# Opening of a windowed-attention and two-layer kernel reordered: sums apart from products, first-layer tiles by pair, scores further ahead, keys loaded first

## The chip, the cores and the metric

One core of one Trainium2 chip. The time is the device time of one execution in microseconds (us), the median of several. `PE` is TensorE, `PEld` its weight loads, `DVE` VectorE, `ACT` ScalarE, `POOL` GpSimd, `SP` the engine that issues most transfers. In the prediction, SWDGE means the transfers that GpSimd issues (here the weights) and HWDGE those that SP issues (here the inputs). PSUM is the memory that TensorE writes its results to (`s`, `x`, `mm`, `ps` and `tp` below are tiles of it).

A line of a timeline gives start and duration in us, engine, line of the kernel, operation, tile written <- tiles read, shapes and number of instructions; in brackets stands how long the engine was idle just before, and what ended that. A line of busy time by stretches gives the stretch, its length, busy time (and instructions) of PE, PEld, DVE, ACT and POOL, the granted TensorE clock, the busy share of the DMA engines, and GB/s.

## The reference

```python
# q, k, v: (8, 8, 576, 64); w_in: (512, 2048); w_out: (2048, 512)
scores = q @ k.transpose(0, 1, 3, 2) / sqrt(64)
scores = where(abs(i - j) <= 32, scores, -1e9)
attn = softmax(scores)
x = (attn @ v).transpose(0, 2, 1, 3).reshape(4608, 512)
h = x @ w_in
out = maximum(0.01 * h, h) @ w_out
```

## The kernel before

A batch is 576 tokens, worked in two halves of 288; a half has four pairs of heads. One *step* is one pair of one half, so steps 0 to 3 are half 0 of batch 0, 4 to 7 its half 1, and 8 is the first of batch 1. A step has scores (five matmuls), an exponential on ACT, a mask product on GpSimd, column sums and weighted values on TensorE, a reciprocal and a scaling on VectorE. The last writes one pair's quarter of `xT`, the input of the first layer. A first-layer tile adds four matmuls, one for each pair.

```python
def weighted(i):                       # before: sums, product and scaling in one piece
    ...
    s = xps.tile([128, HALF], FP32, name="s")      # one buffer
    nc.tensor.matmul(s, ones_bd, ...)              # column sums
    ...
    nc.tensor.matmul(x[:, a:a + n], vbd[b % 2][:, p, blk, :], pr[:, c0:c0 + n], ...)
    ...
    nc.vector.reciprocal(r, s)
    nc.vector.tensor_mul(xT[:, p, t0:t0 + HALF], x, r)

def h_tile(g, f):                      # first layer: one of 16 tiles of a half
    h = mmps.tile([128, 512], FP32, name="mm", tag="mm")        # four buffers
    for c in range(DMC):
        nc.tensor.matmul(h[:, 0:HALF], w_in_bf[:, c, ts(f, 128)], xT[:, c, ds(t0, HALF)], ...)
    nc.scalar.activation(out=gT[:, f, ds(t0, HALF)], in_=h[:, 0:HALF], func=AF.Prelu, alpha=0.01)

# opening
load_qk(0, 0); load_qk(0, 1); load_v(0, 0); load_qk(0, 2); load_v(0, 1); load_qk(0, 3); ...
...
for i in range(NPAIR):
    score(i + 1)
    ...
    if i > 0:
        keep_busy(3 if i == 1 else 2)  # filler matmuls of 512 columns
    weighted(i)
...
for f in range(FFC):                   # first layer of half 0, then of half 1, then second layer
    h_tile(0, f)
    if f in (2, 6, 10):
        step()
```

The softmax here doesn't subtract the row's maximum and nothing guards it: scores larger than these inputs give would overflow.

Of the kernel before, what the change touches and what calls it, by code (L numbers as in the profile page):

```python
# [16 lines left out]
def kernel(  # L17
# [31 lines left out]
    cast = ctx.enter_context(tc.tile_pool(name="cast", bufs=1))  # L49
    attn = ctx.enter_context(tc.tile_pool(name="attn", bufs=2))  # L50
    joined = ctx.enter_context(tc.tile_pool(name="joined", bufs=2))
    kt = ctx.enter_context(tc.tile_pool(name="kt", bufs=4))
    tdma = ctx.enter_context(tc.tile_pool(name="tdma", bufs=1))
# [10 lines left out]
    def load_qk(b, p, behind=None):  # L64


        for into, src, name in ((qf, q, "qf"), (kf, k, "kf")):
            t = fload.tile([96, 2, RUN * D], FP32, name=f"{name}{p}")
            if behind is not None:
                nc.sync.dma_start(out=t[0:1, 0, 0:1], in_=behind.bitcast(FP32))  # L70
                behind = None
            nc.sync.dma_start(  # L72
                out=t, in_=src[b, p:H:NPAIR].rearrange("a (p c) d -> p a (c d)", c=RUN),
            )
            into[b, p] = t

    def load_v(b, p, behind=None):

        t = fload.tile([128, NB, D], FP32, name=f"vf{p}")
        if behind is not None:  # L80
            nc.sync.dma_start(out=t[0:1, 0, 0:1], in_=behind.bitcast(FP32))
        for a in range(2):
            nc.sync.dma_start(  # L83
                out=t[64 * a:64 * a + 64],
                in_=v[b, NPAIR * a + p].rearrange("(c p) d -> p c d", p=64),
            )
        vf[b, p] = t
# [4 lines left out]
    load_qk(0, 2)  # L92
    load_v(0, 1)
    load_qk(0, 3)
    load_v(0, 2)
    load_v(0, 3)

# [27 lines left out]
    clear(vbd[0], 0)  # L125
    clear(vbd[0], 1)


# [11 lines left out]
    for lo in (0, 64):  # L140
        w = win[lo:lo + 64]
        nc.gpsimd.affine_select(
            out=w, in_=w, compare_op=ALU.is_ge, fill=0.0,
            base=0, channel_multiplier=-1, pattern=[[0, 3], [1, 128]],
        )
        nc.gpsimd.affine_select(
            out=w, in_=w, compare_op=ALU.is_ge, fill=0.0,
            base=2 * W, channel_multiplier=1, pattern=[[0, 3], [-1, 128]],
        )
    win_f = win.rearrange("p n c -> p (n c)")  # L150
    mask = [const.tile([128, NCOL], BF16, name=f"mask{i}") for i in range(2)]
# [25 lines left out]
    def cast_qk(b, p, q_eng=None):  # L177
        for eng, src, dst in ((q_eng or nc.gpsimd, qf, qb), (nc.gpsimd, kf, kb)):
            eng.tensor_copy(  # L179
                out=dst[:, p], in_=src[b, p].rearrange("p a (c d) -> p c a d", d=D),  # L180
            )

# [62 lines left out]
    def where(i):  # L245
        return i // 8, (i // 4) % 2, i % 4

    def score(i):
# [14 lines left out]
        nc.gpsimd.tensor_mul(pr, e, mask[hf])  # L263
        probs[i] = pr, None

    def join(i):
# [6 lines left out]
        nc.vector.tensor_add(both, t[:, lo:lo + HALF], t[:, lo + HALF:lo + 2 * HALF])  # L273
        probs[i] = probs[i][0], both

    def weighted(i):
        b, hf, p = where(i)
        pr, both = probs.pop(i)
        x = xps.tile([128, HALF], FP32, name="x")
        s = xps.tile([128, HALF], FP32, name="s")  # L280
        if both is not None:
            nc.tensor.matmul(s, ones_bd, both, start=True, stop=True)  # L282
        else:
# [6 lines left out]
                pr[:, HALF * hf:HALF * hf + NCOL - HALF], start=False, stop=True, skip_group_check=True,  # L290
            )
        c0 = 0
        for n_, (blk, q0, n) in enumerate(WIN[hf]):
# [5 lines left out]
            c0 += n  # L299
        r = attn.tile([128, HALF], FP32, name="r")  # L300
        nc.vector.reciprocal(r, s)  # L301
        t0 = (b * S + hf * HALF) % RING
        nc.vector.tensor_mul(xT[:, p, t0:t0 + HALF], x, r)  # L303



    gT = const.tile([128, FFC, RING], BF16)

    def h_tile(g, f):

        t0 = g * HALF % RING
        h = mmps.tile([128, 512], FP32, name="mm", tag="mm")
        for c in range(DMC):
            nc.tensor.matmul(  # L314
                h[:, 0:HALF], w_in_bf[:, c, ts(f, 128)], xT[:, c, ds(t0, HALF)],
                start=(c == 0), stop=(c == DMC - 1),
            )
        nc.scalar.activation(  # L318
            out=gT[:, f, ds(t0, HALF)], in_=h[:, 0:HALF], func=AF.Prelu, alpha=0.01,
        )  # L320

# [16 lines left out]

    def keep_busy(n):


        t = mmps.tile([128, 512], FP32, name="mm", tag="mm")
        for _ in range(n):
            nc.tensor.matmul(t, ones_bd, mask[0][:, 0:512], start=True, stop=True)

# [24 lines left out]
    def step():  # L370
# [8 lines left out]
        if b > 0:  # L379
            upto = 8 * (b + 1) + (PLAN[b > 1][0][r] if b + 1 < BY_DMA else 0)  # L380
            step_transposes(max(upto - 1, 8 * (b + 1)))
        if i < 7:
            score(i + 1)
        elif 8 <= i < NC - 2:
            nb, _, np_ = where(i + 2)
# [56 lines left out]
    first_pair()  # L442
    clear(vbd[0], 2)
    cast_v(0, 0)
    cast_qk(0, 2, nc.vector)
    score(0)
    load_w_in(0, 512)
    first_pair()
    clear(vbd[0], 3)
    cast_qk(0, 3, nc.vector)  # L450
    load_w_in(512, 1024)
    for i in range(NPAIR):
        score(i + 1)
        if i + 1 < NPAIR:
            cast_v(0, i + 1, on_act=True)
        if i < 2:
            load_w_in(1024 + 512 * i, 1536 + 512 * i)
        else:
            load_w_out(i - 2)
        if i > 0:  # L460
            keep_busy(3 if i == 1 else 2)
        weighted(i)
        if i == 0:
            first_pair()
    state["done"] = NPAIR



    for p in range(NPAIR):
        load_qk(1, p, w_in_bf[0:1, 0, 512:514] if p == 0 else None)  # L470
    keep_busy(2)
    step()
    load_w_out(2)
    load_w_out(3)
    for f in range(FFC):
        h_tile(0, f)
        if f in (2, 6, 10):
            step()
        if f % 4 == 3:
            nc.gpsimd.memset(kbd[1][:, f // 4], 0.0)  # L480
    cast_qk(1, 0, nc.vector)
    cast_qk(1, 1, nc.vector)
    for p in range(NPAIR):
        load_v(1, p, w_out_bf[0:1, 4, 0:2] if p == 0 else None)
    second = transposes(1)
    for f in range(FFC):
        h_tile(1, f)
        if f % 4 == 3:
            p = f // 4
            next(second)  # L490
            next(second)
            place_keys()
            if p + 2 < NPAIR:
                cast_qk(1, p + 2, nc.vector)
            nc.gpsimd.memset(vbd[1][:, p], 0.0)  # L495
        if f == 11:
            score(8)
    state["tp"] = 16
    score(9)

# [25 lines left out]
    def spend(us):  # L526
# [13 lines left out]
        b, p = state["tp"] // 8, state["tp"] % 8 // 2  # L540
        turn += 1
        if kind == "o" and turn % 2 and b >= BY_DMA and (b, p, "k") in qkT and state["done"] > asked[b, p] + 2:
            step_transposes(state["tp"] + 1)
# [38 lines left out]
```

## Time and profile before

| what | value |
|---|---|
| median | 324.78 us (three executions, 324.5 to 325.22) |
| profiled execution | 325.57 us, span 323.9 us |
| TensorE busy, first 28 us | 14.89 us |
| TensorE busy, 28 to 60 us | 31.36 of 32 us |
| first matmul of the first layer | 28.00 us |
| first matmul of the second layer | 48.72 us |

The lines are shown in the prediction. They are read thus: what ends the program is a TensorE that is full from 28 us on, so the question is how much of its work is done by a given moment of the opening.

### The profile page before, as it was taken

The page shows a single profiled execution, that of the slowest core. Times are in us where ns is not written, and L with a number is a line of the kernel's source. Part 1 is how long each engine was busy: PE and PEld are TensorE (multiplying, and loading weights), DVE is VectorE, ACT ScalarE, POOL GpSimd, SP SyncE. Part 2 cuts the span into 40 slices and gives each one's busy share as a digit, 9 for nine tenths or more (in the row PEclk, how much of TensorE's full clock was granted, in tenths as well). Part 3 has the DMA queues.
Part 4 walks back from the last instruction along what each step waited for, and adds up shares of the span by engine and source line. Part 5 has one row for each costly group of instructions (what it writes and reads, how often), then busy time and mean ns, then how long its engine had stood idle before and what let it go on. Part 6 is the DMA issues. An engine that isn't in the chain of part 4 may idle for free.

```text
span 323.9 us, 6543 instructions
## 1 busy us (share of the span) xinstructions
PE 305.0 (94%) x2463; PEld 205.4 (63%) x2485; DVE 208.8 (64%) x260; ACT 224.7 (69%) x432; POOL 180.4 (56%) x213
## 2 busy tenths in 40 slices
PE   2587999999999999999999999999999999999995
PEld 1445784576675766666675767676674857676653
DVE  5489743876757859677848878677838667565100
ACT  5784793376668798788788788888885837464531
POOL 7698739859755877259633796169623644230000
PEclk9999999999999999999999999999999999999999
DMA  8999988899997999919994299827711100010101
GB/s 185 217 195 218 268 209 210 206 237 238 216 203 147 285 192 213 226 67 162 206 216 136 71 221 215 178 83 126 178 38 65 35 33 34 22 46 0 67 32 66
DMA packets 85172, 48.28 MB, mean 149 GB/s; under 512 B 64020, under 2 KB 80660, under 8 KB 85140
## 3 DMA queue, kind: packets, MB, share of 16 engines
q1 hardware_dynamic: 80852, 43.66, 62.5%
q0 software_dynamic: 4288, 4.20, 7.9%
q8 instruction: 19, 0.31, 0.4%
q14 instruction: 13, 0.11, 0.1%
HBM read 36.70 MB, written 9.44 MB: 142 GB/s over the span
## 4 chain that ended last, share of the span: by engine, by line
PE 79%; DMA 7%; DVE 5%; SPq 2%; POOL 2%; ACT 1%; issue 1%; DVEq 0%; ACTq 0%; POOLq 0%
PE mm L331 34%; PE mm L314 34%; DMA kf<-in_k_dram 7%; PE x L295 4%; PE ps L253 4%; DVE r L301 4%; PE s L282 2%; SPq L72 1%; SPq L83 1%; POOL vbd L495 1%; DVE xT L303 1%; PE tp L212 1%; ACT kT L226 1%; POOL kb L179 1%; POOL prob L263 0%
## 5 line engine op out<-in xcount | busy, mean ns | idle before, releaser
L301 DVE RECIPROCAL r<-s 128x288 f32<-128x288 f32 x64 | 125.1, 1955 | 60.0 <-PE s L282 53.7
L314 PE MATMUL mm<-xT,w_in_bf 128*128 128x288 bf16 x1024 | 133.1, 286 | 0.0
L263 POOL TENSOR_TENSOR prob<-e,mask 128x544 bf16<-128x544 bf16 x64 | 77.8, 1216 | 98.7 <-ACT e L259 80.4
L331 PE MATMUL mm<-w_out_bf,gT 128*128 128x512 bf16 (+2 forms) x571 | 128.3, 373 | 1.1
L318 ACT ACTIVATE gT<-mm 128x288 bf16<-128x288 f32 x256 | 104.3, 413 | 23.7 <-PE mm L314 8.1
L314 PEld LDWEIGHTS <-w_in_bf 128*128 128x128 bf16 x1024 | 97.9, 98 | 23.9
L331 PEld LDWEIGHTS <-gT 128*128 128x128 bf16 x592 | 56.0, 98 | 59.8
L336 ACT ACTIVATE o_sb<-mm 128x512 f32<-128x512 f32 (+2 forms) x37 | 21.7, 585 | 55.7 <-PE mm L331 55.7
L259 ACT ACTIVATE e<-ps 128x544 bf16<-128x544 f32 x64 | 39.8, 622 | 11.0 <-PE ps L253 10.5
L238 DVE COPY kbd<-kT 64x576 bf16<-64x576 bf16 x64 | 28.5, 446 | 21.3 <-ACT kT L226 20.5
L189 POOL CAST vbd<-vf 64x576 bf16<-64x576 f32 x58 | 38.6, 666 | 2.2 <-DMA vf<-in_v_dram 0.3
L303 DVE TENSOR_TENSOR xT<-x,r 128x288 bf16<-128x288 f32 x64 | 29.3, 458 | 6.7
L179 POOL CAST kb<-kf 96x768 bf16<-96x768 f32 x32 | 27.5, 860 | 9.6 <-DMA kf<-in_k_dram 9.6
L295 PE MATMUL x<-prob,vbd 128*128 128x128 bf16 (+2 forms) x320 | 26.3, 214 | 1.5 <-DVE xT L303 1.1
L253 PEld LDWEIGHTS <-kbd 128*128 128x128 bf16 x320 | 21.8, 101 | 8.0
L253 PE MATMUL ps<-qT,kbd 128*128 128x128 bf16 (+2 forms) x320 | 26.8, 216 | 0.0
L295 PEld LDWEIGHTS <-vbd 128*128 128x128 bf16 x320 | 21.8, 99 | 5.4 <-issue 1.8
L220 ACT ACTIVATE qT<-qT 128x576 bf16<-128x576 bf16 x20 | 23.6, 1182 | 0.0
L226 ACT ACTIVATE kT<-kT 128x576 bf16<-128x576 bf16 x20 | 23.6, 1179 | 0.0
L273 DVE TENSOR_TENSOR both<-prob 128x288 bf16<-128x288 bf16 x52 | 22.9, 441 | 0.6
L179 POOL CAST qb<-qf 96x768 bf16<-96x768 f32 x24 | 19.8, 825 | 0.0
L282 PE MATMUL s<-both,ones_bd 128*128 128x288 bf16 x52 | 14.9, 286 | 0.0
(40 smaller groups left out, 96.0 us busy)
## 6 DMA issues: line engine op xcount, KB each, us to landing
qf<-in_q_dram SPq DMA_DIRECT2D x32, 288.0 KB, 4.1
kf<-in_k_dram SPq DMA_DIRECT2D x32, 288.0 KB, 5.0
vf<-in_v_dram SPq DMA_DIRECT2D x64, 144.0 KB, 4.7
out_dram<-o_sb SPq DMA_DIRECT2D x35, 256.0 KB, 2.1
w_in_bf<-in_moe_w_in_dram POOLq DMA_DIRECT2D x8, 256.0 KB, 6.7
w_out_bf<-in_moe_w_out_dram POOLq DMA_DIRECT2D x4, 512.0 KB, 14.4
qT<-qb SPq DMA_TRANSPOSE x20, 4.5
kT<-kb SPq DMA_TRANSPOSE x20, 3.7
```

The costliest lines, as they stand in the source:

```text
L179: eng.tensor_copy(out=dst[:, p], in_=src[b, p].rearrange("p a (c d) -> p c a d", d=D),)
L189: nc.gpsimd.tensor_copy(out=vbd[b % 2][r, p, :, r], in_=vf[b, p][r])
L238: nc.vector.tensor_copy(out=kbd[b % 2][r, p, :, r], in_=kT[r].rearrange("p (n j) -> p n j", j=64),)
L253: nc.tensor.matmul(ps[:, c0:c0 + n], kbd[b % 2][:, p, blk], qT[b][:, p, q0:q0 + n], start=True, stop=True,)
L259: nc.scalar.activation(out=e, in_=ps[:, lo:lo + NCOL], func=AF.Exp, scale=scale,)
L263: nc.gpsimd.tensor_mul(pr, e, mask[hf])
L295: nc.tensor.matmul(x[:, a:a + n], vbd[b % 2][:, p, blk, :], pr[:, c0:c0 + n], start=(n_ == 0), stop=(n_ == len(WIN[hf]) - 1), skip_group_c ...
L301: nc.vector.reciprocal(r, s)
L303: nc.vector.tensor_mul(xT[:, p, t0:t0 + HALF], x, r)
L314: nc.tensor.matmul(h[:, 0:HALF], w_in_bf[:, c, ts(f, 128)], xT[:, c, ds(t0, HALF)], start=(c == 0), stop=(c == DMC - 1),)
L318: nc.scalar.activation(out=gT[:, f, ds(t0, HALF)], in_=h[:, 0:HALF], func=AF.Prelu, alpha=0.01,)
L331: nc.tensor.matmul(o[:, lo:hi], gT[:, f, ds(128 * j % RING, 128)], w_out_bf[:, f, lo:hi], start=(f == 0), stop=(f == FFC - 1),)
```

## The change

The intent is to give TensorE useful work earlier. Sums and reciprocals are issued apart from, and ahead of, the products. Scores run up to three steps ahead. The first four tiles of the first layer take the contribution of one pair at a time in four buffers, so three quarters of their work need not wait for the last pair. All keys are loaded before the values of pairs 1 to 3. Batch 1's inputs are issued earlier, and its pairs 2 and 3 are transposed during the second layer.

```diff
-    load_v(0, 1)
     load_qk(0, 3)
-    load_v(0, 2)
-    load_v(0, 3)
+    for p in range(1, NPAIR):
+        load_v(0, p)
...
+    def h_first(g):
+        hs = [mmps.tile([128, 512], FP32, name="mm", tag="mm") for _ in range(4)]
+        yield hs[0]
+        for c in range(DMC):
+            for f in range(4):
+                h_mms(g, f, hs[f], (c,))
+            if c == DMC - 1:
+                for f in range(4):
+                    h_out(g, f, hs[f])
+            yield
...
-            nc.tensor.matmul(t, ones_bd, mask[0][:, 0:512], start=True, stop=True)
+            nc.tensor.matmul(t[:, lo:lo + 224], ones_bd, mask[0][:, 0:224], start=False, stop=False, ...)
...
+    cast_qk(0, 3, nc.scalar)
     load_w_in(0, 512)
+    scaled(0)
+    sums(1)
+    keep_busy(state["ps"], 0, 3)
...
+    def second_half():
+        i = state["done"]
+        weighted(i)
+        if i < 7:
+            sums(i + 1)
+        if i < 5:
+            score(i + 3)
+        state["done"] += 1
+    for f in range(4, FFC):
+        h_tile(0, f)
+        if f in (7, 10, 13):
+            second_half()
...
+        if turn == 1:
+            second_pair(2)
+        if turn == 2:
+            score(9)
+        if turn == 4:
+            second_pair(3)
```

More of the change, by code (lines that the diff above doesn't have):

```diff
@@ L50 @@
     attn = ctx.enter_context(tc.tile_pool(name="attn", bufs=2))
+    kt = ctx.enter_context(tc.tile_pool(name="kt", bufs=4))
     joined = ctx.enter_context(tc.tile_pool(name="joined", bufs=2))
-    kt = ctx.enter_context(tc.tile_pool(name="kt", bufs=4))
+    recip = ctx.enter_context(tc.tile_pool(name="recip", bufs=3))
     tdma = ctx.enter_context(tc.tile_pool(name="tdma", bufs=1))
@@ L69, in load_qk @@
             if behind is not None:
-                nc.sync.dma_start(out=t[0:1, 0, 0:1], in_=behind.bitcast(FP32))
+                behind.memset(t[0:1, 0, 0:1], 0.0)
                 behind = None
@@ L75, in load_qk, with load_v @@
             into[b, p] = t
-    def load_v(b, p, behind=None):
+    def load_v(b, p):
         t = fload.tile([128, NB, D], FP32, name=f"vf{p}")
-        if behind is not None:
-            nc.sync.dma_start(out=t[0:1, 0, 0:1], in_=behind.bitcast(FP32))
         for a in range(2):
@@ L126 @@
     clear(vbd[0], 1)
+    clear(vbd[0], 2)
     PAD = 32
@@ L149 @@
         )
+    nc.gpsimd.memset(vbd[0][:, 3], 0.0)
     win_f = win.rearrange("p n c -> p (n c)")
@@ L178, in cast_qk @@
         for eng, src, dst in ((q_eng or nc.gpsimd, qf, qb), (nc.gpsimd, kf, kb)):
-            eng.tensor_copy(
-                out=dst[:, p], in_=src[b, p].rearrange("p a (c d) -> p c a d", d=D),
-            )
+            tok = src[b, p].rearrange("p a (c d) -> p c a d", d=D)
+            if eng is nc.scalar:
+                eng.activation(out=dst[:, p], in_=tok, func=AF.Copy)
+            else:
+                eng.tensor_copy(out=dst[:, p], in_=tok)
     def cast_v(b, p, on_act=False):
@@ L263, in score @@
         nc.gpsimd.tensor_mul(pr, e, mask[hf])
-        probs[i] = pr, None
+        probs[i] = [pr, None, None]
+        state["ps"] = ps
     def join(i):
@@ L273, in join, with sums @@
         nc.vector.tensor_add(both, t[:, lo:lo + HALF], t[:, lo + HALF:lo + 2 * HALF])
-        probs[i] = probs[i][0], both
-    def weighted(i):
+        probs[i][1] = both
+    def sums(i):
         b, hf, p = where(i)
-        pr, both = probs.pop(i)
-        x = xps.tile([128, HALF], FP32, name="x")
+        pr, both, _ = probs[i]
         s = xps.tile([128, HALF], FP32, name="s")
@@ L291, in weighted, with product @@
             )
+        r = recip.tile([128, HALF], FP32, name="r")
+        nc.vector.reciprocal(r, s)
+        probs[i][2] = r
+    def product(i):
+        b, hf, p = where(i)
+        pr = probs[i][0]
+        x = xps.tile([128, HALF], FP32, name="x")
         c0 = 0
@@ L299, in weighted, with place, scaled, h_mms @@
             c0 += n
-        r = attn.tile([128, HALF], FP32, name="r")
-        nc.vector.reciprocal(r, s)
+        probs[i][1] = x
+    def place(i):
+        b, hf, p = where(i)
         t0 = (b * S + hf * HALF) % RING
-        nc.vector.tensor_mul(xT[:, p, t0:t0 + HALF], x, r)
+        return xT[:, p, t0:t0 + HALF]
+    def scaled(i):
+        _, x, r = probs.pop(i)
+        nc.vector.tensor_mul(place(i), x, r)
+    def weighted(i):
+        if probs[i][2] is None:
+            sums(i)
+        product(i)
+        scaled(i)
     gT = const.tile([128, FFC, RING], BF16)
-    def h_tile(g, f):
-        t0 = g * HALF % RING
-        h = mmps.tile([128, 512], FP32, name="mm", tag="mm")
-        for c in range(DMC):
+    def h_mms(g, f, h, cs):
+        for c in cs:
             nc.tensor.matmul(
-                h[:, 0:HALF], w_in_bf[:, c, ts(f, 128)], xT[:, c, ds(t0, HALF)],
+                h[:, 0:HALF], w_in_bf[:, c, ts(f, 128)], xT[:, c, ds(g * HALF % RING, HALF)],
                 start=(c == 0), stop=(c == DMC - 1),
             )
+    def h_out(g, f, h):
         nc.scalar.activation(
-            out=gT[:, f, ds(t0, HALF)], in_=h[:, 0:HALF], func=AF.Prelu, alpha=0.01,
+            out=gT[:, f, ds(g * HALF % RING, HALF)], in_=h[:, 0:HALF], func=AF.Prelu, alpha=0.01,
         )
+    def h_tile(g, f):
+        h = mmps.tile([128, 512], FP32, name="mm", tag="mm")
+        h_mms(g, f, h, range(DMC))
+        h_out(g, f, h)
+    def h_first(g):
[8 more added lines that the diff above has]
+            yield
     def o_tile(j, hook=None):
@@ L337, in o_tile, with keep_busy @@
             nc.sync.dma_start(out=out[ts(j, 128), lo:hi], in_=o_sb[:, lo:hi])
-    def keep_busy(n):
-        t = mmps.tile([128, 512], FP32, name="mm", tag="mm")
+    def keep_busy(t, lo, n):
         for _ in range(n):
-            nc.tensor.matmul(t, ones_bd, mask[0][:, 0:512], start=True, stop=True)
+            nc.tensor.matmul(
+                t[:, lo:lo + 224], ones_bd, mask[0][:, 0:224], start=False, stop=False,
+                skip_group_check=True,
+            )
     NC = 2 * NPAIR * B
@@ L381, in step @@
             step_transposes(max(upto - 1, 8 * (b + 1)))
-        if i < 7:
-            score(i + 1)
-        elif 8 <= i < NC - 2:
+        if 8 <= i < NC - 2:
             nb, _, np_ = where(i + 2)
@@ L442 @@
     first_pair()
-    clear(vbd[0], 2)
     cast_v(0, 0)
+    score(0)
     cast_qk(0, 2, nc.vector)
-    score(0)
+    score(1)
+    sums(0)
+    next(first)
+    next(first)
+    product(0)
+    keep_busy(state["ps"], 0, 2)
+    place_keys()
+    cast_qk(0, 3, nc.scalar)
     load_w_in(0, 512)
-    first_pair()
-    clear(vbd[0], 3)
-    cast_qk(0, 3, nc.vector)
+    scaled(0)
+    sums(1)
+    keep_busy(state["ps"], 0, 3)
     load_w_in(512, 1024)
-    for i in range(NPAIR):
-        score(i + 1)
-        if i + 1 < NPAIR:
-            cast_v(0, i + 1, on_act=True)
-        if i < 2:
-            load_w_in(1024 + 512 * i, 1536 + 512 * i)
-        else:
-            load_w_out(i - 2)
-        if i > 0:
-            keep_busy(3 if i == 1 else 2)
-        weighted(i)
-        if i == 0:
-            first_pair()
@@ L465 @@
-    state["done"] = NPAIR
-    for p in range(NPAIR):
-        load_qk(1, p, w_in_bf[0:1, 0, 512:514] if p == 0 else None)
-    keep_busy(2)
-    step()
+    next(first)
+    score(2)
+    next(first)
+    cast_v(0, 1, on_act=True)
+    load_w_in(1024, 1536)
+    place_keys()
+    keep_busy(state["ps"], 0, 8)
+    sums(2)
+    score(3)
+    load_w_in(1536, 2048)
+    product(1)
+    scaled(1)
+    cast_v(0, 2, on_act=True)
+    score(4)
+    h0 = h_first(0)
+    h = next(h0)
+    keep_busy(h, HALF, 8)
@@ L473 @@
+    product(2)
+    scaled(2)
+    sums(3)
+    cast_v(0, 3, on_act=True)
+    load_w_out(0)
+    for p in range(NPAIR):
+        load_qk(1, p, nc.gpsimd if p == 0 else None)
+    for p in range(NPAIR):
+        load_v(1, p)
+    next(h0)
+    next(h0)
+    score(5)
+    load_w_out(1)
+    product(3)
+    next(h0)
+    scaled(3)
+    sums(4)
+    next(h0)
+    score(6)
     load_w_out(2)
     load_w_out(3)
-    for f in range(FFC):
-        h_tile(0, f)
-        if f in (2, 6, 10):
-            step()
-        if f % 4 == 3:
-            nc.gpsimd.memset(kbd[1][:, f // 4], 0.0)
+    state["done"] = NPAIR
@@ new lines, in second_half, with second_pair @@
+    def second_half():
[7 more added lines that the diff above has]
+    for f in range(4, FFC):
+        h_tile(0, f)
+        if f in (7, 10, 13):
+            second_half()
+        if f % 2 == 1:
+            nc.gpsimd.memset((kbd if f < 12 else vbd)[1][:, (f - 4) // 2 % 4], 0.0)
+    second = transposes(1)
+    def second_pair(p):
+        next(second)
+        next(second)
+        place_keys()
+        if p + 2 < NPAIR:
+            cast_qk(1, p + 2, nc.vector)
@@ L481 @@
+    second_half()
     cast_qk(1, 0, nc.vector)
     cast_qk(1, 1, nc.vector)
-    for p in range(NPAIR):
-        load_v(1, p, w_out_bf[0:1, 4, 0:2] if p == 0 else None)
-    second = transposes(1)
-    for f in range(FFC):
+    for _ in h_first(1):
+        pass
+    for f in range(4, FFC):
         h_tile(1, f)
-        if f % 4 == 3:
-            p = f // 4
-            next(second)
-            next(second)
-            place_keys()
-            if p + 2 < NPAIR:
-                cast_qk(1, p + 2, nc.vector)
-            nc.gpsimd.memset(vbd[1][:, p], 0.0)
-        if f == 11:
+        if f in (7, 11):
+            second_pair((f - 7) // 4)
+        if f in (7, 9):
+            nc.gpsimd.memset(vbd[1][:, (f - 3) // 2], 0.0)
+        if f == 13:
@@ L497 @@
             score(8)
     state["tp"] = 16
-    score(9)
     H_US, O_US, LEAD = 4 * (HALF / 2400 + 2.5e-3), 4 * 0.216, 4.0
```

## The prediction

> **What bounds the kernel now.** I read the page first for busy shares, then the busy time by stretches, to see where TensorE is not full.
>
> ```profile
> PE 305.0 (94%) x2463; PEld 205.4 (63%) x2485; DVE 208.8 (64%) x260; ACT 224.7 (69%) x432; POOL 180.4 (56%) x213
> ...
> PE   2587999999999999999999999999999999999995
> ```
> ```profile
> 0.00:28.00 28.00, 14.89 (x121) 9.70 (x123) 18.45 (x29) 18.09 (x25) 22.82 (x37) 1.00 1.11 200
> 28.00:60.00 32.00, 31.36 (x287) 22.32 (x286) 19.43 (x23) 20.92 (x48) 24.07 (x27) 1.00 0.95 220
> 60.00:100.00 40.00, 39.64 (x351) 27.29 (x353) 29.00 (x36) 25.41 (x55) 27.62 (x33) 1.00 1.05 221
> ...
> 320.00:324.00 4.00, 0.39 (x8) 0.22 (x4) 0.00 (x0) 0.35 (x2) 0.00 (x0) 0.87 0.20 68
> ```
>
> Second column: length; then PE busy. From 28 us to 320 us TensorE is idle about 2.3 us in all, part of that from missing records. So a microsecond by which useful TensorE work gets ahead before 28 us, or in the next 20, comes off the end, provided no new wait appears. Only the opening has slack: 13.1 us idle, and its 14.89 busy us include nine keep-busy matmuls of 512 columns (line 344) and slow-clock matmuls.
>
> Next I read the timeline of the opening, for the first product of the first layer and for the chain ahead of it.
>
> ```profile
> 20.05 1.96 DVE L301 RECIPROCAL r<-s 128x288 f32<-128x288 f32 x1 [0.69 <-PE s L288]
> ...
> 22.11 0.46 DVE L303 TENSOR_TENSOR xT<-x,r 128x288 bf16<-128x288 f32 x1
> ...
> 22.73 1.96 DVE L301 RECIPROCAL r<-s 128x288 f32<-128x288 f32 x1 [0.17 <-PE s L288]
> ...
> 27.25 0.46 DVE L303 TENSOR_TENSOR xT<-x,r 128x288 bf16<-128x288 f32 x1
> ...
> 28.00 1.63 PE L314 MATMUL mm<-xT,w_in_bf 128*128 128x288 bf16 x12
> ```
>
> The path is reciprocal, scaling, next reciprocal: about 2.46 us a step on VectorE (1.96 + 0.46 + waits). All four pairs must have passed before tile 0 is begun at 28.00. From there TensorE runs without a break to the second layer, which starts at 48.72. The work between: 128 first-layer matmuls at 0.122 (16 of them span 2.12, of which about 0.16 is the last one's drain) = 15.6, four sets of transposes at 0.47 = 1.9, sums and products of steps 5-7 at 0.49 = 1.5, scores 6-9 at 0.23 = 0.9: 19.9 of the 20.72 elapsed. Warm TensorE is the bound there.
>
> The other limit is data. The waits up to 60 us:
>
> ```profile
> POOL kb L179 <- DMA kf<-in_k_dram: 9.6, 7, 3.2
> ...
> PE s L284 <- DVE r L301: 2.2, 3, 1.1
> ...
> PE x L295 <- POOL vbd L189: 0.3, 1, 0.3
> ```
>
> The last keys of batch 0 land at 16.06, those of batch 1 at 47.2 (chain of waits), with the DMA busy share near or above one from 4 to 45 us.
>
> **What the Trainium skill says.** (1) "TensorE: Matmul & The Clock Gate", Part 1: the array runs at half rate until about 3.4 us of sustained activity. The trace agrees: transposes-to-products groups of 544 columns take 0.65 us up to 22.3 us and 0.40 from 22.6. So filler matmuls matter, and their number is rightly reduced to what keeps the window full. (2) "PSUM — Partial Sum Buffer", Four PSUM rules, rule 2: a starting matmul clears the flags of its whole bank, so two open accumulation groups cannot share one. Hence four banks for tiles 0-3 by pair, all four of the product pool. No run yet shows this. (3) Same page, "Engine vs sequencer instructions": the other engines' queues are strict FIFO. The trace agrees: the first exponential's scores were ready at 10.0 but it began at 11.19, behind a key copy and a 1.15 us clear. (4) "DMA: Bandwidth & Descriptors", SWDGE vs HWDGE: the two kinds use different queues served round-robin, so weights and inputs share. The trace agrees in kind: between 16 and 30 us the weights' queue took 108% and the input queue 16% of engine time.
>
> **The change, part by part.** I walk the new program order of each engine with durations from the old trace: reciprocal 1.96, scaling 0.46, mask product 1.22, exponential 0.62, transposed copy 0.65, value cast on ACT 0.69 a half, pair placement 0.91, a GpSimd weight issue pair about 1.25 to 1.4.
>
> *First scores.* The third clear moves to the front and the fourth to GpSimd (1.06 us, in the wait for the first keys, 1.13 us). exp 0 starts at 10.25 instead of 11.19, its mask product ends about 12.1 instead of 14.14. Sums 0 follow at once, so reciprocal 0 starts at 12.8 instead of 15.82.
>
> *All keys first.* Between k2 (12.14) and k3 (16.06) the old order moved 0.885 MB, 0.226 MB/us; without v1's 0.295 MB, k3 lands at about 14.75: 1.3 earlier. Its cast ends at 15.6. The last query's cast on ACT (estimated 0.80 from the slope between 544 and 1152 elements) needs no VectorE gap.
>
> *Price on GpSimd.* The first weight issue moves from 14.09 to about 15.6, behind that cast; the second ends at 18.3. With issue-to-landing of 5.8 to 8.3 us the first chunk is there at about 22.8; its first use is at about 23.25. Mask product 2 queues behind these issues (18.3 to 19.55).
>
> *VectorE chain.* Placement and scaling 0 hold reciprocal 1 to 16.25; mask product 2 holds reciprocal 2 to 20.2; then scaling 1 ends 22.66, scaling 2 at 23.65, reciprocal 3 at 25.6, scaling 3 at 26.06. Old: scaling 3 ended at 27.71. So xT of pair 3 is 1.65 us earlier.
>
> *Tiles 0-3 by pair.* Pairs 0 to 2, 12 matmuls = 1.48 us, run in gaps before 25.5; after 26.1 only four remain. Tile 4 starts when ACT has freed its bank, about 26.95, with tiles 0-3, scores 0-6, sums 0-4 and products 0-3 done. Work left up to the second layer, with everything in: 28 tiles 13.7, products 4-7 0.98, sums 5-7 0.72, scores 7-9 0.7, transposes 1.88 = 18.0, so about 45.0 against 48.72: a gain of 3.7 if TensorE never waits.
>
> *It will wait.* Steps 4-7 are now spaced three tiles apart. Reciprocal 5 starts at 29.8 (product 4 sits behind tile 7), ends 31.8; sums 6 reaches TensorE at 31.4: 0.45 lost. Reciprocal 6 ends 34.23, sums 7 reaches at 33.8: 0.48 lost. xT of pair 3 for half 1 is then at 37.15 (old 38.07), which the by-pair opening of group 1 hides: its last round starts at 37.2. All four outputs then start together, so tile 4 waits for ACT about 0.3. Sum of losses 1.2, gain 3.7 - 1.2 = 2.5. The old 0.26 us wait for values at 54.8 should go, since batch 1's values no longer wait behind a token read of the weights: about +0.2. Total 2.7.
>
> *Batch 1's data.* Pairs 2 and 3 and score 9 move into the second layer's turns. At about 45.1 second layer starts; pair 3 is due at 48.4; k3 lands at 47.2 or a little sooner (loads start at 26 instead of 27.2), cast by 48.05. That just fits. Products 8 come due at 51.5, values cast by about 50.7. Nothing further is removed after this; instruction totals there are the same.
>
> 324.78 - 2.7 = 322.1 us.
>
> **Rivals.** *A, no wait takes over:* gain 3.7 to 4, time 320.9. For: 2.3 us idle in 292 shows how well the steady part hides things. Against: the reciprocal's 1.96 us is fixed and `s` has one bank. *B, data:* weights are issued 1.5 us later. If chunk 1 lands at 25 rather than 22.8, the first three rounds slip to after 25 and 0.5 to 1.5 us go; if chunk 4 (issued at 22.5, up to 8.3 us) or k3 of batch 1 is late, as much again: 323.5. For: shares above one. Against: SWDGE kept 108% in that stretch. *C, clock:* filler is shorter and has gaps near 19 and 21 us; were the array slow up to 25, products and two rounds would take twice their time, about 1.4 lost: 323.5. Against: the old array was warm at 22.6 after similar gaps. *D, GpSimd:* mask products, weight issues and six clears run nearly back to back to 39 us; mask product 7 ends at 34.1 just as sums 7 wants it, and the first key cast of batch 1 ends at 40.15, transposes wanting it at 40.2. A slip of 0.5 passes straight on: 322.6.
>
> **Range and chances.** The plain walk says 322.1; hand walks miss small hops, so B to D weigh on the slow side and A on the fast: 320.8 to 323.6. Faster by over 2% would need a gain of 6.5 us, more than the 3.7 + 0.3 that the work count permits plus half of everything idle: 0.02. Slower by over 2% needs a new stall of 9 us: 0.01. Within 2%: 0.97.
>
> **What would show it.** Right: reciprocal 0 near 12.8; first-layer matmuls from about 23.3 in groups of four; tile 4 near 27; two waits of sums for a reciprocal of about 0.5 each between 31 and 35; second layer near 45; busy share after 60 us unchanged. Wrong: first-layer matmuls waiting for w_in; a 544-column group of 0.65 us after 23 us; TensorE waiting for GpSimd's kb or prob between 34 and 52; the lead at 45 us lost again by 55.

## The result

The changed kernel took 323.19 us (median of four, 322.6 to 323.95) against 325.0 us for the kernel before in the same rounds. The ratio is 0.9947, 95% interval 0.9922 to 0.9973: the same within 2%, but clear of one. A ratio here is the mean time of one kernel's fast runs over that of the other's of the same rounds, so it is not quite the ratio of the medians.

The page of the changed kernel, TensorE's busy time and its digits over the span:

```profile
PE 303.9 (95%) x2476; PEld 205.9 (64%) x2497; DVE 212.7 (66%) x259; ACT 223.6 (70%) x432; POOL 182.3 (57%) x215
...
PE   2779999999999999999999999999999999999995
```

Busy time by stretches, columns as before:

```profile
0.00:28.00 28.00, 17.33 (x166) 13.12 (x167) 20.34 (x28) 20.22 (x33) 25.15 (x40) 1.00 1.10 198
28.00:60.00 32.00, 30.25 (x271) 20.69 (x273) 24.07 (x24) 18.89 (x44) 26.29 (x29) 1.00 1.07 243
60.00:100.00 40.00, 39.79 (x351) 27.43 (x354) 27.55 (x37) 26.39 (x56) 26.12 (x31) 1.00 1.07 217
```

The opening holds 2.4 us more of busy TensorE (filler and matmuls at the slow rate count as busy too). The stretch from 28 to 60 us, which was nearly full, has lost 1.1 us again. After 60 us nothing differs. The timeline of the opening shows both, the gain and the new waits:

```profile
12.77 1.96 DVE L296 RECIPROCAL r<-s 128x288 f32<-128x288 f32 x1 [0.29 <-PE s L291]
...
22.40 1.14 PE L336 MATMUL mm<-xT,w_in_bf 128*128 128x288 bf16 x8
...
26.09 2.12 PE L336 MATMUL mm<-xT,w_in_bf 128*128 128x288 bf16 x16
...
30.87 0.30 PE L287 MATMUL s<-prob,ones_bd 128*128 128x288 bf16 x1 [0.24 <-DVE r L296]
...
32.42 1.14 PE L336 MATMUL mm<-xT,w_in_bf 128*128 128x288 bf16 x8 [0.66 <-DMA w_in_bf<-in_moe_w_in_dram]
...
49.18 2.75 PE L373 MATMUL mm<-w_out_bf,gT 128*128 128x512 bf16 x12 [0.46 <-DMA w_out_bf<-in_moe_w_out_dram]
```

The first reciprocal starts at 12.77 us in place of 15.82. Two rounds by pair (eight matmuls) run at 22.40, and tile 4 starts at 26.09. Then TensorE waits: for a reciprocal at 30.87, for the last quarter of `w_in` at 32.42, for the last chunk of `w_out` at 49.18. The last two are waits that the kernel before did not have.

I follow the difference with a *lead*: how much earlier a step's scores start than the same step's in the profiled execution before. From step 11 on, the lead is constant in every run, so what is lost is lost before then; that constant value is what the expectations call the lead at score 10. For the changed kernel it is 2.56 us. That execution before was 0.6 us slower than the median of four, so leads are good for comparing traces and are somewhat too large as gains.

### The profile page after: what moved, and what is told of

Same layout as the page of the kernel before. It is cut to its first block, busy times and chain, and to the rows that moved or that the text cites. A ratio compares the mean times of both kernels' runs of the same rounds, so it can differ in the third digit from the quotient of the medians.

```text
span 321.3 us, 6563 instructions
## 1 busy us (share of the span) xinstructions
PE 303.9 (95%) x2476; PEld 205.9 (64%) x2497; DVE 212.7 (66%) x259; ACT 223.6 (70%) x432; POOL 182.3 (57%) x215
## 4 chain that ended last, share of the span: by engine, by line
PE 79%; POOL 6%; DMA 6%; DVE 4%; ACT 3%; issue 2%; POOLq 0%; DVEq 0%; ACTq 0%
PE mm L373 35%; PE mm L336 33%; DMA w_out_bf<-in_moe_w_out_dram 6%; PE x L307 4%; PE ps L255 4%; DVE r L296 2%; PE s L285 2%; POOL prob L265 2%; POOL kb L183 1%; ACT kT L228 1%; DVE xT L322 1%; PE tp L214 1%; POOL w_in_bf L465 1%; ACT e L261 1%; ACT gT L342 0%
## 5 line engine op out<-in xcount | busy, mean ns | idle before, releaser
L240 DVE COPY kbd<-kT 64x576 bf16<-64x576 bf16 x64 | 28.5, 445 | 16.3 <-ACT kT L228 15.6
L183 POOL CAST kb<-kf 96x768 bf16<-96x768 f32 x32 | 28.6, 895 | 2.6 <-DMA kf<-in_k_dram 2.6
L255 PEld LDWEIGHTS <-kbd 128*128 128x128 bf16 x320 | 21.5, 99 | 10.2 <-DVE kbd L240 1.4
L307 PEld LDWEIGHTS <-vbd 128*128 128x128 bf16 x320 | 21.4, 99 | 3.9 <-DVE xT L322 1.0
## 6 DMA issues: line engine op xcount, KB each, us to landing
w_out_bf<-in_moe_w_out_dram POOLq DMA_DIRECT2D x4, 512.0 KB, 16.3
```

What stands on the lines that cost most here:

```text
L183: eng.tensor_copy(out=dst[:, p], in_=tok)
L240: nc.vector.tensor_copy(out=kbd[b % 2][r, p, :, r], in_=kT[r].rearrange("p (n j) -> p n j", j=64),)
L255: nc.tensor.matmul(ps[:, c0:c0 + n], kbd[b % 2][:, p, blk], qT[b][:, p, q0:q0 + n], start=True, stop=True,)
```

## The experiments

I held two theories of why the lead is 2.6 us and not the 3.7 that the work count allowed at tile 4. **Chain**: sums wait for reciprocals on VectorE, and the data waits only coincide with that. **Data**: weights land late because batch 1's inputs now share the transfer engines with them from 25 us on. The rest of the runs undo one part of the change each. Every kernel got six executions; the lead is of its one trace.

| run | median us | before us | ratio (95%) | lead us |
|---|---|---|---|---|
| a0 | 323.05 | 325.59 | 0.9915 (0.9887 to 0.9942) | 2.02 |
| no_batch1_loads (wrong result) | 322.38 | 325.59 | 0.9898 (0.9873 to 0.9923) | 2.85 |
| cheap_recip (wrong result) | 322.90 | 325.59 | 0.9915 (0.9890 to 0.9941) | 2.75 |
| v1_late | 323.08 | 325.59 | 0.9922 (0.9897 to 0.9947) | 2.51 |
| both_off (wrong result) | 322.46 | 325.78 | 0.9896 (0.9878 to 0.9914) | 3.22 |
| whole_tiles | 324.60 | 325.78 | 0.9960 (0.9930 to 0.9990) | 0.75 |
| steps_early | 322.92 | 325.78 | 0.9905 (0.9882 to 0.9928) | 2.84 |
| steps_early_keys_later | 322.13 | 325.78 | 0.9877 (0.9855 to 0.9898) | 3.30 |
| v_before_keys | 324.48 | 325.05 | 0.9971 (0.9948 to 0.9993) | 0.11 |
| sums_with_products | 324.63 | 325.05 | 0.9973 (0.9954 to 0.9991) | 0.69 |
| no_filler | 323.76 | 325.05 | 0.9950 (0.9931 to 0.9969) | 1.01 |
| pairs_early | 323.25 | 325.05 | 0.9935 (0.9915 to 0.9955) | 2.27 |

The groups of four rows were run together, on one chip each; compare medians within a group, ratios between groups. The changed kernel's own two ratios, 0.9947 and 0.9915, are 0.0032 apart (1 us), so differences of that size between groups are not resolved.

**a0: nothing edited.**

> The changed kernel again, nothing edited, for a second trace and a tighter interval. Chain theory (the lead that the work count allows, 3.7 us at tile 4, shrinks to 2.6 because sums wait for reciprocals on VectorE) and data theory (it shrinks because weights land late behind batch 1's earlier inputs: 0.66 us wait for w_in, 0.46 us for w_out) both say 323.2 us, within 0.5, and a lead of 2.0 to 2.6 us over the kernel before at score 10. If the lead in this trace differs from 2.57 by more than 0.3, the data theory says that the two DMA waits differ by that, the chain theory that the waits for reciprocals do.

323.05 us, so the gain in these rounds is 2.5 us in place of 1.8. The trace, in its timeline:

```profile
26.93 2.12 PE L336 MATMUL mm<-xT,w_in_bf 128*128 128x288 bf16 x16
...
31.71 0.30 PE L287 MATMUL s<-prob,ones_bd 128*128 128x288 bf16 x1 [0.24 <-DVE r L296]
...
32.80 1.14 PE L336 MATMUL mm<-xT,w_in_bf 128*128 128x288 bf16 x8 [0.20 <-DMA w_in_bf<-in_moe_w_in_dram]
...
49.73 2.75 PE L373 MATMUL mm<-w_out_bf,gT 128*128 128x512 bf16 x12 [0.37 <-DMA w_out_bf<-in_moe_w_out_dram]
```

Tile 4 starts 0.84 us later than in the first trace, and the lead is only 0.54 smaller, chiefly because the wait for `w_in` shrank by 0.46: it ends at nearly the same moment, 32.4 and 32.8. The difference at tile 4 goes back to the last key, whose cast on GpSimd started at 14.28 us in the first trace and at 15.15 here. So one and the same kernel opens 0.9 us apart, by when its last key lands. Neither theory had that, and their test in this run decides for neither. The two data waits do differ, by 0.55 us together, but the wrong way: they are shorter where the lead is smaller. The waits for reciprocals hardly differ (0.14 us more). What the run shows is that the wait at `w_in` ends when the chunk lands (32.29 and 32.66 us), whenever TensorE arrives.

**no_batch1_loads: batch 1 reuses batch 0's inputs.**

```diff
     def load_qk(b, p, behind=None):
+        if b == 1:
+            qf[1, p], kf[1, p] = qf[0, p], kf[0, p]
+            return
     def load_v(b, p):
+        if b == 1:
+            vf[1, p] = vf[0, p]
+            return
```

> Batch 1 reuses batch 0's float inputs (wrong result on purpose), so its 3.5 MB do not share the DMA engines with the weights. Data theory: both DMA waits vanish, the lead at score 10 rises from 2.57 to about 3.7 and the time falls by 1.1, to 322.1 us. Chain theory: the w_in wait is replaced by waits of sums 6 and 7 for the reciprocal (0.3 to 0.5 each), the lead stays under 3.1, the time at or above 322.6 us.

The time is 322.38 us, 0.67 below a0, and the lead 2.85. Both data waits are gone. Waits for reciprocals stand in the place of the `w_in` wait:

```profile
31.32 0.30 PE L292 MATMUL s<-prob,ones_bd 128*128 128x288 bf16 x1 [0.24 <-DVE r L301]
...
33.78 0.30 PE L292 MATMUL s<-prob,ones_bd 128*128 128x288 bf16 x1 [0.34 <-DVE r L301]
```

The second of these is new against the first trace of the changed kernel. The lead is what the chain theory said; the time lies between the two expectations.

**cheap_recip: the reciprocals of steps 4 to 7 as copies.**

```diff
-        nc.vector.reciprocal(r, s)
+        if 4 <= i < 8:
+            nc.vector.tensor_copy(out=r, in_=s)
+        else:
+            nc.vector.reciprocal(r, s)
```

> The reciprocals of steps 4 to 7 become copies out of PSUM (wrong result on purpose), some 1.4 us shorter each. Chain theory: 0.5 us or more faster than the changed kernel, 322.6 us or less. Data theory: only the 0.24 us wait at step 6 is at stake and the w_in wait takes it over; time within 0.2 us of the changed kernel, and the w_in wait is 0.8 us or more.

322.90 us, 0.15 below a0, the same ratio: the data theory was right on the time. TensorE had no wait for a reciprocal and reached the second layer at 44.54 us, a full microsecond before no_batch1_loads (45.55), both from tile 4 at 26.54. At `w_in` it lost 0.28 us (the chunk landed at 31.78), not the 0.8 that I had written. It then stood still at `w_out`:

```profile
49.00 2.75 PE L376 MATMUL mm<-w_out_bf,gT 128*128 128x512 bf16 x12 [0.95 <-DMA w_out_bf<-in_moe_w_out_dram]
```

The chunk lands near 49 us (TensorE goes on at 49.18, 49.73 and 49.00 in three traces), whether TensorE comes early or not. With the inputs of batch 1 not loaded it landed at 40.74. These two runs show two limits in series. Lifting one alone mostly uncovers the other.

**v1_late: batch 1's values behind group 0's last step.**

```diff
-    for p in range(NPAIR):
-        load_v(1, p)
...
     second_half()
+    for p in range(NPAIR):
+        load_v(1, p)
```

> Batch 1's values are issued after group 0's last step (some 35 us) and not right behind its keys. Data theory: the 0.46 us wait for w_out goes, 0.3 to 0.5 us faster (322.8 us) unless values then hold products 8. Chain theory: no change beyond 0.2 us. If the values' own order is what kept the lead, products 8 wait for the value cast, and the time is 323.5 us or more.

323.08 us, no change against a0. The trace has no wait for `w_out`, but that does not show that the values hold it up: the last chunk took 18.9 us from issue to landing, in steps_early, with the values late too, 19.3, and with the values early 19.6 (first trace) and 19.3 (a0). It landed at 48.99, and TensorE wanted it only at 49.23. The waits for reciprocals grew, as without the loads, and TensorE then waited 0.32 us for a query cast of pair 2. The data expectation of 0.3 to 0.5 us was a miss.

**both_off: the first two together.**

> Both limits away: batch 1 reuses batch 0's inputs and the reciprocals of steps 4 to 7 are copies (wrong on purpose). Alone, the first gave 322.4 us and a lead of 2.86, the second 322.9 and 2.76. If chain and data are two limits in series, each hiding the other, the lead at score 10 becomes 3.6 us or more (2.86 plus 0.9 of waits for reciprocals) and the time about 321.5 us. If either alone were the whole cause, this is no better than the better of the two: 322.3 us and a lead near 2.9.

A miss: 322.46 us, no better than no_batch1_loads in time, and a lead of 3.22, not 3.6. Neither a reciprocal nor data is listed among the waits of the trace (sums 7 still came 0.14 us late). TensorE waited at batch 1's first transposes instead:

```profile
39.05 0.43 PE L219 MATMUL tp<-ident,qb 96*128 96x96 bf16 x6 [0.55 <-DVE qb L188]
...
39.73 0.43 PE L219 MATMUL tp<-ident,kb 96*128 96x96 bf16 x6 [0.25 <-POOL kb L188]
```

The query casts on VectorE and the key cast on GpSimd come late, by the trace because GpSimd is clearing buffers for batch 1 until 37.5 us; no run moves those clears alone. This is a third limit, hidden behind the other two; the prediction's rival D had put it at 40.2 us.

**whole_tiles: tiles 0 to 3 not by pair.**

```diff
-            for f in range(4):
-                h_mms(g, f, hs[f], (c,))
             if c == DMC - 1:
                 for f in range(4):
+                    h_mms(g, f, hs[f], range(DMC))
                     h_out(g, f, hs[f])
```

> Tiles 0 to 3 of both groups in whole tiles, all 16 matmuls after the last pair's xT, nothing else undone. If the rounds by pair carry the gain, group 0 and group 1 each lose up to 12 matmuls of 0.122, 1.5 us: 2.9 us less the up to 1.1 of data waits that this absorbs, so 325.0 to 326.0 us, no better than before. If the earlier scores and sums carry it, the loss is under 1 us: 324.0 or less.

324.60 us, ratio 0.9960; the lead falls to 0.75. By the ratios about half of a0's gain goes with this part (0.0045 of 0.0085), less than the 2 to 3 us expected; the time lies between the two expectations. In group 1 all work waits for the last pair:

```profile
38.40 3.71 PE L336 MATMUL mm<-xT,w_in_bf 128*128 128x288 bf16 x29 [1.02 <-DVE xT L322]
```

**steps_early and steps_early_keys_later.** Both have batch 1's values late as in v1_late and these edits:

```diff
-        if f in (7, 10, 13):
+        if f in (5, 9, 13):
             second_half()
-        if f % 2 == 1:
-            nc.gpsimd.memset((kbd if f < 12 else vbd)[1][:, (f - 4) // 2 % 4], 0.0)
+        if f % 2 == 1 and f < 12:
+            nc.gpsimd.memset(kbd[1][:, (f - 4) // 2], 0.0)
...                                     # in group 1's tile loop
+        if f in (4, 5):
+            nc.gpsimd.memset(vbd[1][:, f - 4], 0.0)
```

The second also issues batch 1's queries and keys behind `score(5)`, not ahead of it.

> Batch 1's values late, the steps of half 1 behind tiles 5, 9, 13 in place of 7, 10, 13, and two clears moved behind batch 1's first casts. Chain theory: VectorE no longer idles 1.3 us before reciprocal 5, so 0.7 us or more faster than the changed kernel: 322.3 or less. Data theory: tile 12 now waits 0.8 us or more for the last chunk of w_in (it lands near 32.4 whatever TensorE does), and the time is 322.7 to 323.2 us.

> The same, and batch 1's queries and keys issued behind mask product 5, 1.2 us later, so that the weights have the DMA engines for longer. Data theory: the wait for w_in shrinks by about half of the 1.2 us, and the time falls to about 322.3 us, 0.5 us below steps_early. Chain theory: no difference between the two beyond 0.2 us.

steps_early took 322.92 us, within the data theory's range: it waited before tile 12, idle for 0.46 us (0.63 from start to start; 0.8 had been expected), and 0.33 us for `w_out`. The profile puts the first down to ACT, but it was `w_in`: ACT was done with tile 8, whose buffer tile 12 takes, at 29.86, while the last chunk of `w_in` landed at 31.68 and TensorE went on at 31.82, the same 0.14 behind the landing as in the first trace and in a0. With the keys later as well it took 322.13 us, 0.8 lower, ratio 0.9877; the data theory said 322.3. Neither weight nor reciprocal is listed among the waits of more than 0.2 us any more:

```profile
44.66 1.03 PE L373 MATMUL mm<-w_out_bf,gT 128*128 128x512 bf16 x4
...
48.10 0.43 PE L214 MATMUL tp<-ident,kb 96*128 96x96 bf16 x6 [0.18 <-POOL kb L183]
...
48.45 2.75 PE L373 MATMUL mm<-w_out_bf,gT 128*128 128x512 bf16 x12
```

Its tile 4 started at 26.74 us, later than in the first trace of the changed kernel, and yet the second layer starts 0.56 us earlier and the last quarter of the second layer's first tile 0.73 us earlier. It is correct, and the fastest of all kernels run here. By the median it beats a0 by 0.9 us, in other rounds; the ratios' intervals overlap (its upper end is 0.9898, a0's lower end 0.9887), so I call that likely rather than shown.

**v_before_keys: load order undone.**

```diff
+    load_v(0, 1)
     load_qk(0, 3)
-    for p in range(1, NPAIR):
+    for p in range(2, NPAIR):
         load_v(0, p)
```

> Only the load order undone: the values of pair 1 again before the last query and key. The last key should land 1.3 us later, and GpSimd's weight issues and mask product 2 with it, so tile 4 moves from 26.1 to 26.9 to about 27.5 to 28. Chain theory: all of it ends in the time, 324.0 to 324.4 us. Data theory: the wait for w_out, near 49.5 whatever TensorE does, absorbs some 0.5 of it: 323.5 to 323.9 us. If the keys' order is idle: 323.1 us.

324.48 us, ratio 0.9971. By the ratios the order of loads carries about as much as the tiles by pair (0.0056 of 0.0085; the intervals overlap). GpSimd in the timeline, here and then in the changed kernel:

```profile
17.01 0.82 POOL L184 CAST kb<-kf 96x768 bf16<-96x768 f32 x1 [2.38 <-DMA kf<-in_k_dram]
```
```profile
14.28 0.82 POOL L183 CAST kb<-kf 96x768 bf16<-96x768 f32 x1
```

The last key is not 1.3 us later but 2.7 (1.9 against a0's trace). Weight issues and mask product 2 follow it on GpSimd, which passes the delay on unchanged: sums 2 start at 21.70 in place of 19.00 (19.84 in a0). From there to tile 4, at 29.49, it grew by 0.7 us, to 3.4 (2.6 against a0). In that stretch TensorE still ran at its slow rate, up to 25.3 us (five score matmuls at 22.11 took 0.66 us, the changed kernel's at 19.23 took 0.40), and the longer matmuls and filler add up to these 0.7. The cost shrank again in the end, as no data wait was left. The profiled execution was this kernel's slowest (325.48), so the sizes are at the large end.

**sums_with_products.**

```diff
         weighted(i)
-        if i < 7:
-            sums(i + 1)
...
     scaled(3)
-    sums(4)
```

> Sums of steps 4 to 7 are again issued with their products, so each reciprocal begins only after its own step. No sums then wait for a reciprocal (0.4 to 0.9 us saved), but reciprocal 7 begins after tile 15, near 35.2, and the xT that group 1 needs last comes at about 37.9 in place of 36.7: 1.1 us lost there. Chain theory: 0.3 to 0.7 us slower than the changed kernel, 323.4 to 323.8 us. Data theory: the w_out wait absorbs it, within 0.2 us of 323.1.

324.63 us, ratio 0.9973, well beyond both expectations. I had counted on no sums waiting for a reciprocal; sums 7 did, since reciprocal 6 itself came later, and the last pair of half 1 was scaled by 39.23 us, 2.5 after the 36.73 of the changed kernel:

```profile
36.26 0.30 PE L287 MATMUL s<-prob,ones_bd 128*128 128x288 bf16 x1 [0.52 <-DVE r L296]
...
39.28 2.90 PE L336 MATMUL mm<-xT,w_in_bf 128*128 128x288 bf16 x20 [0.59 <-DVE xT L322]
```

**no_filler: no keep-busy matmuls** (`range(n)` becomes `range(0)`).

> No keep-busy matmuls at all. If the array's clock needs them to be full by 23 us, groups of 544 columns still take 0.65 us after 23 us and tile 4 comes 1 us or more later: 324 us or more. If the useful work alone fills the clock's window, within 0.3 us of the changed kernel, 323.1 us.

323.76 us, ratio 0.9950: about 1.1 us slower than a0 by the ratios, but level with the changed kernel's first set (0.9947). Neither expectation named this time. In the trace, of this kernel's slowest execution, matmuls stayed slow into the first-layer rounds:

```profile
23.43 2.13 PE L336 MATMUL mm<-xT,w_in_bf 128*128 128x288 bf16 x8
```

Eight matmuls took 2.13 us, where the changed kernel's took 1.14; tile 4 came at 28.70. They reached the full rate only at about 28.2 us, after 5.6 us of nearly unbroken matmuls from 22.55 us on, longer than the 3.4 us that the prediction counted with (0.240 us a matmul of 288 columns before, 0.123 after). The granted clock that the profile lists reads 1.00 from 23 to 28 us all the same, so the slow rate is seen in the durations alone. Without filler the full rate comes later and tile 4 with it; what that is worth in time, 0 to 1.1 us, these rounds do not settle.

**pairs_early: batch 1's pairs 2 and 3 in group 1 again.**

```diff
-        if f in (7, 11):
-            second_pair((f - 7) // 4)
+        if f in (6, 9, 12, 15):
+            second_pair((f - 6) // 3)
...
-        if turn == 1:
-            second_pair(2)
-        if turn == 4:
-            second_pair(3)
```

> Batch 1's pairs 2 and 3 are transposed again between tiles of group 1 (behind tiles 6, 9, 12 and 15) and not in the second layer's turns. If batch 1's keys land near 41.5 and 45.5 as in the changed kernel, TensorE waits 1 to 1.5 us for the last pair, and the w_out wait shrinks by as much as half a microsecond: 323.8 to 324.3 us. If the deferral bought nothing: 323.1 us.

323.25 us, ratio 0.9935 between the changed kernel's two (0.9947 and 0.9915). The deferral bought nothing that these rounds can see. TensorE did wait, 0.88 us, though for pair 2's query cast on VectorE, not for pair 3's keys:

```profile
43.82 0.43 PE L214 MATMUL tp<-ident,qb 96*128 96x96 bf16 x6 [0.88 <-DVE qb L183]
```

In return the wait for `w_out` vanished, as the second layer then starts later.

## Why the prediction was right or wrong

The measured 323.19 and 323.05 us lie within 320.8 to 323.6, and "within 2%" holds. The point, 322.1, was too fast by about one microsecond: a gain of 2.7 was forecast, and 1.8 and 2.5 were measured in the two sets of rounds.

*What held.* Reciprocal 0 at 12.8 came at 12.77. First-layer matmuls ran in rounds before tile 4, from 22.40 on. "Tile 4 near 27" was 26.09 and 26.93, "second layer near 45" 45.22 and 45.85. The busy share after 60 us did not change (39.64 and 39.79 of 40). Of the two waits for reciprocals the first came where stated. Undoing the tiles by pair, the load order, or the early sums gave medians of 324.5 to 324.6 us against 323.05 and 323.19, and left leads of 0.1 to 0.8 us, so each of these steps carries weight. How much is less certain: half to two thirds of the gain by a0's ratio, a quarter to a half by the first set's. The load order was forecast to bring the last key 1.3 us earlier; against the kernel before (16.06) it landed 2.0 us earlier in the first trace (14.11) and 1.0 in a0 (15.09).

*What failed: "It will wait", the sum of losses of 1.2 us.* I measure each loss from start to start, less the streaming time of the matmuls between.

| loss after tile 4, us | predicted | first trace | a0 |
|---|---|---|---|
| sums 6 for reciprocal 5 | 0.45 | 0.40 | 0.40 |
| tile 12 for `w_in` | 0 | 0.82 | 0.36 |
| sums 7 for reciprocal 6 | 0.48 | 0 | 0.14 |
| group 1's rounds and its tile 4 (tile 4 alone, for ACT: 0.29 in both) | 0.3 | 0.50 | 0.36 |
| pair 2's transposes | 0 | 0 | 0.23 |
| last quarter of the second layer's first tile, for `w_out` | 0 | 0.62 | 0.54 |
| sum | 1.2 | 2.3 | 2.0 |

The waits for the chain were sized right, and the `w_in` wait swallowed the second of them. The term that was left out is data: 1.44 us and 0.90 us. The prediction had it as rival B and gave it no share of the 1.2. Rival B asked whether the first chunk of `w_in` would come in time (it did, at 20.86 us) and whether batch 1's last key would (it did, cast at 45.06). It also asked about the fourth chunk of `w_in`, and allowed it up to 8.3 us from an issue at 22.5. That is where it was wrong: the chunk took 10.0 us (22.25 to 32.29) and 9.6 in a0, against 8.1 in the kernel before. Batch 1's queries and keys were walked from 26 us on, but issued from 24.95; their last key landed 2.3 us earlier than walked (44.94, not 47.2), and the weights later than in the kernel before. The argument "SWDGE kept 108% in that stretch" was taken from a stretch in which batch 1's inputs had hardly begun. The landings of `w_in` and then of `w_out`, each before and then after:

```profile
DMA to landing us min/median/max: 5.8/6.7/8.3
DMA to landing us min/median/max: 4.5/7.9/10.0
...
DMA to landing us min/median/max: 10.4/14.4/18.5
DMA to landing us min/median/max: 12.9/16.3/19.6
```

`w_out` it did not ask about at all, though its median from issue to landing, 14.4 us before, was on the page; its last chunk, issued at 29.5 and sharing the engines with batch 1's inputs, landed some 20 us later. Even so it landed only 1.5 us later than in the kernel before, where it took 18.5 us (to 47.64) and was wanted at about 51.3 (an estimate: 12 matmuls of 0.216 us after 48.72). In the changed kernel TensorE wanted it at 48.56. So the larger part of this wait is that TensorE came 2.8 us earlier for a chunk that is late in both kernels.

Two of the prediction's own signs of being wrong came true: first-layer matmuls waited for `w_in`, and the lead of 3.5 us at the start of the second layer (45.22 against 48.72) was 2.57 by 55 us.

*What made up for part of it.* The step "values in time, +0.2" gave 0.44: the lead goes from 2.13 at step 10's scores to 2.57 at the next. And tile 4 in the first trace was 0.86 earlier than walked. Most of that is the spread of the loads: in a0 it came as walked, though a0's last key was cast some 0.3 us later than walked, so the walk was a little slow as well. That the time stayed in the range despite the missing term is thus in part luck.

*A reading that does not hold.* The prediction calls the filler shorter and its number reduced. Counted in columns there is slightly more of it: 21 matmuls of 224 columns (4704) against nine of 512 (4608). What changed is where it stands, from 14.14 us on instead of about 18. Matmuls ran at the full rate from 16.3 us in the first trace and from 16.0 in a0, against 22.6 before. Rival C did not come true, but the moment is not fixed: in runs with the same opening it lies between 16.0 and about 21.5 us (21.4 in sums_with_products, whose tile 4 came at 26.95 like a0's). How much of the gain comes from the earlier full rate no run separates.

*What stays open.* The median gain in the two sets of rounds differs by 0.7 us, most of it in the kernel before (325.0 and 325.59). The landing of the last key varies by 1.0 us between two traces of the changed kernel; whether the kernel before varies likewise was not traced. Which part of batch 1's inputs delays the weights is told in part. For `w_out` the inputs as a whole are shown to: its last chunk took 10.8 and 11.2 us from issue to landing in the two traces without them, and 15.7 to 19.6 in the others. For `w_in` the values hardly can (in the first trace they were issued from 31.08 us on, and it landed at 32.29), and that the queries and keys do is likely, not shown. Its last chunk took 7.9 and 8.3 us without the loads, 7.6 with the queries and keys later, and 8.8 to 10.0 in six traces in which they follow it by 2.7 us. But in four others, in which they follow it by 2.7 us too (whole_tiles, sums_with_products, no_filler, v_before_keys), it took 6.9 to 8.7.

## What to carry to other kernels

When work is pulled forward, list every later consumer of a transfer again with its new time, not only the ones next to the edit: here the wait moved to weights that are used 20 us after the last edited line. Two or three limits can stand in series within a microsecond of each other, so removing one in an experiment shows only the next; remove them in pairs before naming the cause. A queue in front of the path (GpSimd's casts, weight issues and mask products) passes a late key on in full, and by these rounds the order of loads was worth about as much as the tiles by pair.

## What the Trainium skill lacked or had wrong

- "SBUF — State Buffer", Who interferes with whom, says that in VectorE's two-port modes, which a cast can enter, VectorE and GpSimd contend: whichever issues first holds the shared ports for its whole instruction and the other blocks. The runs agree in kind, but the page has no size for a chain: one query cast of 96x768, 0.56 us in the median before, took 2.26 us beside two GpSimd clears in a row (2.05 us together), so it did not get in between them. In both_off two such casts took 5.43 us, beside three clears and two key casts, and held TensorE up for 0.55.
- "DMA: Bandwidth & Descriptors", Anatomy of one DMA, gives 2.0 us plus bytes over 436 GB/s for a DMA from GpSimd. For a `w_in` transfer that reads 0.5 MB this is about 3.2 us (an estimate from that page); the medians were 6.7 us before and 7.9 us after, and 14.4 and 16.3 us for `w_out`, with the engines shared. The page has no figure for a loaded queue, and the term that the prediction missed is of that kind.
- No page that I used has the spread of landings between executions of one program: the last key's cast began at 14.28 us in one and at 15.15 us in another.
